# One core, windowed attention into a SoLU layer: the same 736 steps, issued in another order with other buffers and engines

## The chip, the core and the metric

The kernel runs on one core of one Trainium2 chip. The metric is the device time of one execution in microseconds (us). The core has a matrix engine (TensorE, written PE), a vector engine (VectorE, DVE), a scalar engine (ScalarE, ACT), a general engine (GpSimd, POOL) and SyncE (SP), which here only issues transfers. The engines run side by side; each takes its own instructions strictly in the order in which the program issues them, and they wait for each other by semaphores.

## The reference

Four batches of eight heads, 768 tokens, head size 64. Each query sees the keys of the last 96 positions and the first 8 keys, with a bias that falls with the distance at a slope of its own for each head. The result (3072 tokens by 512) goes through a layer whose activation is h times softmax(h), then a layer norm with gain g, then a second matrix.

```python
scores = q @ k.T / 8 - slope[h] * dist          # where kept: rel in [0, 96) or key < 8
a = softmax(scores);  x = a @ v                 # x: 3072 x 512 after joining the heads
h = x @ w_in                                    # 512 -> 1024
solu = h * softmax(h)
ln = (solu - mean(solu)) / sqrt(var(solu) + 1e-6) * g_ln
out = ln @ w_out                                # 1024 -> 512, float32
```

## The kernel before

**The plan.** The kernel first collects numbered steps in a `Plan`. A step is a Python function that issues a few instructions, with the buffers that it takes. 736 of them stand in the order of issue. Four lists, written out in the source, then fix everything that is free. `ORDER` is the order of issue, and so the order on each engine. `SLOTS` gives the index of each buffer that a step takes from a ring: 7 float32 landing buffers (`x32_`), 4 float16 ones (`x16_`), 3 and 2 for v, 5 each for the transposed q and k (`qT`, `kT`), 12 for the exponentials (`eb`), 4 for the activations (`uu`), 6 for the transposed activations (`late`), 3 output buffers (`osb`) and 8 PSUM banks (`acc`), which are taken singly or in pairs. `ENGS` names the engine of each step that may run on more than one: casts, evacuations of PSUM, squares, output scaling. `WARM` lists dummy matmuls as position:bank:count: ahead of that place of `ORDER`, so many 128x512 matmuls on a constant tile (`busy`, L1220) go to PE. Waits between engines follow from who writes and reads each buffer, so a buffer that is taken again waits for its last reader.

**The attention.** For each batch, pairs of heads of q and k come in as float32 (`load_heads` L472, `load_rows` L479), are cast to float16 (helper: ACT L266, DVE L268, POOL L270), transposed on PE (L728) and evacuated into `qT` and `kT` by the same helper. Only in batch 3 are the transposes made by DMA (L762). v comes in by `load_v` (L486) and is cast; the eight global keys' values are placed into a sparse tile `vgz` by POOL (L508), the global keys into `kg` (L516). The scores of 64-row blocks with their windows are PE work (L874, with the bias matmul L860), ACT takes the exponential (L882), some pairs are multiplied by a factor tile afterwards on DVE or POOL (`fac`, L890, two float16 operands). The scores of the global keys (L933) and their exponentials (L940) run beside that. Column sums come from PE (L954, L963), a logarithm on ACT (L970), the spread over the heads from PE (L1009), the reciprocals `rr` from an exponential on ACT (L1018). Then PE forms the weighted sums of v (L1043 for the global keys, L1053 for the windows, together called av below), DVE copies one column as a mark (`tick` L1063) and multiplies with `rr` into `xT` (L1078).

**The layer.** For each tile of 128 tokens, 24 in all: the first product (GEMM1, L1112, eight matmuls of 128x512 into a pair of banks), its exponential on ACT with the sum (`ef`, L1118), the product with h on DVE (`u`, L1121), the square with its sum on ACT (L1128) or DVE (L1132), the transpose of u, by DMA (`uturn`, L1137) or by PE (L1147), the statistics in small steps (L1167 to L1176), the second product (GEMM2, L1193, eight matmuls), its scaling on ACT (L1204) or DVE (L1207), and the store (L1211).

**The weights.** `w_in` and `w_out` come in as four transfers each (L610, L620). `w_in` is cast; `w_out` is multiplied by g (L633 to L639), its mean is formed by PE (L646) and taken away (L650).

**The queue.** All transfers, the DMA transposes among them, are issued by SP in the order of `ORDER`, so a transfer that waits for its buffer or its data holds up all behind it; only two stores at the very end are issued by ACT. A few more small steps build constant tiles at the start.

Names of steps used below: 480 is the load of a pair of q heads of batch 2; 645 is the last DMA transpose of batch 3's q and 941 the DMA transpose of an activation tile that follows it; 655 and 665 are two of the last v loads; 598 is a cast of k; 529 and 206 are exponentials of scores; 345 is a score step; 854 is one GEMM1 and 889 the exponential `ef` of another; 678 and 690 are score steps and 693 and 716 global-score steps of batch 3; 958 is a GEMM2 and 978 a GEMM1.

Of the kernel before, what the change touches and what calls it, by code (L numbers as in the profile page):

```python
# [29 lines left out]
FACT = {1, 2, 3}  # L30
SPLIT = False
ORDER = """
# [30 lines left out]
"""  # L63
SLOTS = """
# [10 lines left out]
"""  # L75
ENGS = """
# [4 lines left out]
"""  # L81
WARM = """
25:0:16 30:2:4 37:3:2 48:5:3 59:3:2 117:7:4 156:6:5
"""


# [1172 lines left out]
```

## Time and profile before

| what | value |
|---|---|
| times of three runs | 154.17, 155.07, 155.03 us |
| median | 155.03 us |
| span of the profiled execution | 154.3 us |
| PE busy | 144.9 us (94%) |
| ACT busy | 123.4 us (80%) |
| DVE busy | 119.2 us (77%) |
| POOL busy | 60.0 us (39%) |
| bytes moved | 36.35 MB in 76429 packets |

The profile is one execution on the core, and every duration below is from it. The median of the runs lies 0.7 us above its span. Times in the timeline count from the start of the span. "x8" at a row means that eight instructions in a line are shown as one; a note in brackets says how long the engine sat idle before it and which instruction or transfer ended that; "SPq" rows are the issues of SP's queue, not the transfers themselves. PE's rows are matmuls; its weight loads (PEld) run beside them.

### The profile page before, as it was taken

The page shows a single profiled execution, that of the slowest core. Times are in us where ns is not written, and L with a number is a line of the kernel's source. Part 1 is how long each engine was busy: PE and PEld are TensorE (multiplying, and loading weights), DVE is VectorE, ACT ScalarE, POOL GpSimd, SP SyncE. Part 2 cuts the span into 40 slices and gives each one's busy share as a digit, 9 for nine tenths or more (in the row PEclk, how much of TensorE's full clock was granted, in tenths as well). Part 3 has the DMA queues.
Part 4 walks back from the last instruction along what each step waited for, and adds up shares of the span by engine and source line. Part 5 has one row for each costly group of instructions (what it writes and reads, how often), then busy time and mean ns, then how long its engine had stood idle before and what let it go on. Part 6 is the DMA issues. An engine that isn't in the chain of part 4 may idle for free.

```text
span 154.3 us, 4774 instructions
## 1 busy us (share of the span) xinstructions
PE 144.9 (94%) x1877; PEld 77.9 (50%) x1877; DVE 119.2 (77%) x241; ACT 123.4 (80%) x212; POOL 60.0 (39%) x145
## 2 busy tenths in 40 slices
PE   6988899999899999799999999999999999999991
PEld 2545556477554565644544644544445644444451
DVE  6749988899999994789799959399893885799200
ACT  3959999799999888499999887878885676884642
POOL 7574456565394626852813115454212000110000
PEclk9999999999999999999999999999999999999999
DMA  4999999999996997999999999998999954488743
GB/s 146 373 305 337 307 391 327 347 340 398 295 264 108 242 285 175 220 270 233 262 196 154 271 141 244 171 233 161 189 231 259 247 141 97 90 222 223 224 166 136
DMA packets 76429, 36.35 MB, mean 236 GB/s; under 512 B 65456, under 2 KB 71928, under 8 KB 76408
## 3 DMA queue, kind: packets, MB, share of 16 engines
q1 hardware_dynamic: 76120, 35.54, 95.0%
q10 hardware_dynamic: 288, 0.52, 0.9%
q8 instruction: 14, 0.23, 0.7%
q14 instruction: 7, 0.06, 0.1%
HBM read 23.15 MB, written 6.29 MB: 191 GB/s over the span
## 4 chain that ended last, share of the span: by engine, by line
PE 44%; DMA 19%; ACT 9%; DVE 8%; POOL 7%; SPq 5%; issue 5%; POOLq 0%; DVEq 0%; ACTq 0%
PE acc L1193 16%; PE acc L1112 15%; DMA v<-in_v_dram 6%; DMA x<-in_q_dram 5%; DMA qT<-x 4%; PE acc L1053 3%; DMA kT<-x 3%; SPq L486 3%; ACT eb L882 2%; POOL x L270 2%; PE acc L728 2%; PE acc L874 2%; DVE uu L1121 2%; ACT ef L1118 2%; ACT rr L1018 1%
## 5 line engine op out<-in xcount | busy, mean ns | idle before, releaser
L1112 PE MATMUL acc<-w_in_sb,xT 128*128 128x512 f16 x192 | 44.4, 379 | 0.0
L1193 PE MATMUL acc<-gw_out_sb,late 128*128 128x512 f16 (+1 forms) x200 | 44.3, 371 | 0.1
L1121 DVE SCALAR_TENSOR_TENSOR uu<-ef,acc 128x1024 f16<-128x1024 f16 x24 | 29.2, 1216 | 5.4 <-ACT ef L1118 5.0
L882 ACT ACTIVATE eb<-acc 128x896 f16<-128x896 f32 (+1 forms) x32 | 29.3, 960 | 1.8 <-PE acc L874 1.8
L1193 PEld LDWEIGHTS <-late 128*128 128x128 f16 x200 | 18.9, 98 | 21.1 <-issue 0.9
L1118 ACT ACTIVATE ef<-acc 128x1024 f16<-128x1024 f32 x24 | 24.8, 1035 | 5.8 <-PE acc L1112 5.4
L1112 PEld LDWEIGHTS <-xT 128*128 128x128 f16 x192 | 18.1, 98 | 21.3 <-issue 1.1
L270 POOL CAST x<-x 128x768 f16<-128x768 f32 x17 | 14.4, 851 | 22.8 <-DMA x<-in_q_dram 7.8
L1078 DVE TENSOR_TENSOR xT<-acc,rr 128x384 f16<-128x384 f32 x32 | 16.3, 549 | 3.6 <-ACT rr L1018 1.9
L1053 PE MATMUL acc<-eb,v 64*64 64x160 f16 (+4 forms) x448 | 16.5, 221 | 2.1 <-DVE xT L1078 1.6
L1053 PEld LDWEIGHTS <-v 64*64 64x64 f16 x448 | 12.9, 106 | 6.6 <-issue 4.3
L1128 ACT ACTIVATE sqa<-uu 128x1024 f16<-128x1024 f16 x15 | 16.1, 1071 | 0.0
L1018 ACT ACTIVATE rr<-acc 128x768 f32<-128x768 f32 x16 | 12.7, 809 | 4.1 <-DVE tick L1063 2.5
L890 DVE TENSOR_TENSOR eb<-eb,fb 128x896 f16<-128x896 f16 (+1 forms) x19 | 14.1, 769 | 0.8 <-ACT eb L882 0.8
L270 POOL CAST v<-v 128x704 f16<-128x704 f32 (+3 forms) x13 | 8.8, 685 | 10.0 <-DMA v<-in_v_dram 9.3
L1220 PE MATMUL acc<-busy 128*128 128x512 f16 x36 | 10.8, 443 | 1.5 <-DVE busy L545 1.5
L728 PE MATMUL acc<-ident,x 128*128 128x128 f16 x144 | 11.1, 220 | 0.8 <-ACT x L266 0.7
L874 PE MATMUL acc<-qT,kT 64*64 64x160 f16 (+2 forms) x384 | 11.4, 227 | 0.3 <-ACT qT L266 0.3
L1132 DVE SCALAR_TENSOR_TENSOR sqv<-uu 128x1024 f16<-128x1024 f16 x9 | 11.5, 1277 | 0.1
L890 POOL TENSOR_TENSOR eb<-eb,fb 128x960 f16<-128x960 f16 (+1 forms) x5 | 10.4, 2081 | 2.0 <-ACT eb L882 2.0
L1043 PE MATMUL acc<-eg,vgz 64*64 64x384 f16 x64 | 10.8, 324 | 0.0
L268 DVE CAST x<-x 128x768 f16<-128x768 f32 x8 | 5.6, 709 | 6.7 <-POOL slr L371 2.3
(120 smaller groups left out, 205.7 us busy)
## 6 DMA issues: line engine op xcount, KB each, us to landing
x<-in_q_dram SPq DMA_DIRECT2D x16, 384.0 KB, 6.0
x<-in_k_dram SPq DMA_DIRECT2D x16, 384.0 KB, 5.1
out_dram<-osb SPq DMA_DIRECT2D x12, 256.0 KB, 4.7
v<-in_v_dram SPq DMA_DIRECT2D x12, 192.0 KB, 4.0
out_dram<-x SPq DMA_DIRECT2D x9, 256.0 KB, 2.2
late<-in_moe_w_in_dram SPq DMA_DIRECT2D x4, 512.0 KB, 7.4
w_out<-in_moe_w_out_dram SPq DMA_DIRECT2D x4, 512.0 KB, 6.0
v<-in_v_dram SPq DMA_DIRECT2D x12, 160.0 KB, 4.0
```

The source lines that it names most:

```text
L270: nc.gpsimd.tensor_copy(out=out, in_=in_)
L874: nc.tensor.matmul(out=sc[o : o + 64, par, col : col + n], lhsT=kk[r, BLK * c : BLK * c + BLK], rhs=qq[r, g0 : g0 + n], start=fresh, stop= ...
L882: ex["fn"] = (lambda ex=ex, qk=qk, gw=gw: nc.scalar.activation(out=eb[at(qk, "eb")][:, :, 0:gw], in_=big(qk)[:, :, 0:gw], func=AF.Exp, sca ...
L890: (nc.gpsimd if fx["at"] == "POOL" else nc.vector).tensor_tensor(out=e, in0=e, in1=fb[:, p, :, 0:gw], op=ALU.mult)
L1018: re["fn"] = lambda re=re, sp_=sp_, w=w: nc.scalar.activation(out=rr[at(re, "rr")][:, :, 0:w], in_=big(sp_)[:, :, 0:w], func=AF.Exp, scale ...
L1053: nc.tensor.matmul(out=o_[64 * h : 64 * h + 64, gl : gl + m], lhsT=vv[r, v_at(vi, h, c), pair, :], rhs=view(eb[at(e_own[b, gi, pair], "eb" ...
L1078: nc.vector.tensor_tensor(out=xT[at(xt_own[b], "xT")][:, p, q0:q1], in0=one(av, d)[:, 0:w], in1=rr[at(re, "rr")][:, d, 0:w], op=ALU.mult)
L1112: nc.tensor.matmul(out=ph()[:, ts(fh, 512)], lhsT=xT[at(xt_own[b], "xT")][:, j, ts(t % NA, P)], rhs=w_in_sb[:, j, ts(fh, 512)], start=(j = ...
L1118: ex["fn"] = lambda g1=g1, t=t, ph=ph: nc.scalar.activation(out=ef[at(g1, "ef")], in_=ph(), func=AF.Exp, accum_out=s0[:, t : t + 1])
L1121: u["fn"] = lambda u=u, g1=g1, t=t, ph=ph: nc.vector.scalar_tensor_tensor(out=uu[at(u, "uu")], in0=ef[at(g1, "ef")], scalar=USC, in1=ph(), ...
L1128: nc.scalar.activation(out=sqs_["ACT"], in_=uu[at(u, "uu")], func=AF.Square, scale=float(D_FF) ** 0.5, accum_out=s2[:, t : t + 1])
L1193: nc.tensor.matmul(out=one(g2)[:, 0:wd], lhsT=uT[at(el_o, "uT")][:, c, :], rhs=gw_out_sb[:, c, sl_], start=(c == 0), stop=(c == NFC - 1))
```

## The change

`ORDER`, `SLOTS`, `ENGS` and `WARM` are replaced; every step and every function stays. The set of steps in `ORDER` is the same. The first 61 steps of SP's queue come in the same order as before; behind these the queue is ordered anew, and so is everything on the other engines.

Decoded, the new lists give: steps on DVE 174 (176 before), on ACT 158 (158), on POOL 82 (79), on SP 140 (141; a third store goes to ACT's queue), on PE 177 (177). By kind, DVE/ACT/POOL, before and after: casts of v 4/4/12 and 0/4/16, casts of q 6/3/7 and 4/2/10, casts of k 2/4/10 and 5/2/9, casts of `w_in` 2/2/4 and 3/2/3, squares 9/15 and 8/16 (DVE/ACT), output scalings 10/15 and 11/14 (DVE/ACT), statistics 2/6 and 4/4 (DVE/POOL). Of the `fac` steps, four go from POOL to DVE (356, 509, 518, 683) and four from DVE to POOL (521, 530, 686, 692). The dummy matmuls are 32 instead of 36; five stood directly ahead of the first GEMM1 and four ahead of the first spread, where none stand now.

```diff
 ORDER = """
-126 86 12 11 271 2 13 17 16 10 15 66 14 18 0 20 73 36 3 75 7 1 4 88 68 69 89 22 53 55 56 90 8 70 38
...
-655 690 865 679 677 689 693 694 691 692 680 978 980 981 975 913 945 958 959 652 695 696 947 697 716
...
-1036 1041 1066 1037 1057 1042 1043 988 1050 1069 1070 989 990 1077 1078 1079 1071 1072 1073 952 953
-1083 1084 954 1085 1088 1089 1090
+86 66 6 73 36 53 38 79 28 18 11 2 88 52 12 10 271 3 115 60 117 92 110 5 99 13 17 15 14 0 4 9 75 279 105
...
+686 673 946 947 693 716 717 689 694 677 674 678 679 680 690 691 692 958 959 978 980 695 913 981 696 917
...
+1028 1036 1037 1065 1050 1042 1043 871 1069 1030 1031 1083 1070 1084 1078 1079 1072 1073 1085 1088 1089
+1090
 """
 SLOTS = """
-0 1 2 3 4 5 0 0 1 2 0 0 1 1 2 0 0 1 3 3 1 2 4 2 2 3 4 0 5 1 2 5 6 3 0 0 1 3 3 1 2 1 0 2 2 3 3 1 1 4
...
+3 5 0 1 2 1 2 0 1 2 4 6 0 3 3 3 0 1 0 2 1 5 7 0 2 0 2 3 4 0 5 1 2 1 4 0 4 3 3 0 2 3 0 1 1 5 1 1 0 7 2 3 7
...
 """
 ENGS = """
-1 0 0 1 1 1 1 1 2 0 2 1 0 0 2 0 1 0 1 0 0 0 1 2 2 2 1 1 2 0 0 1 1 1 1 0 1 2 2 0 2 1 2 1 0 1 0 0 1 1
...
+1 0 1 1 1 0 1 1 2 0 2 1 2 0 0 0 1 0 0 0 0 0 1 1 2 0 0 2 1 0 2 1 1 0 1 0 2 2 1 2 0 0 0 1 1 1 0 1 1 0 1 0 1
...
 """
 WARM = """
-25:0:16 30:2:4 37:3:2 48:5:3 59:3:2 117:7:4 156:6:5
+24:0:3 25:0:16 66:2:4 70:2:5 106:6:4
 """
```

75 rows, old and new, of tables (ENGS, ORDER, SLOTS) are left out of this document.

## The prediction

> **What bounds the kernel now.** I read the page first: span, busy time, slices, chain.
>
> ```profile
> span 154.3 us, 4774 instructions
> PE 144.9 (94%) x1877; PEld 77.9 (50%) x1877; DVE 119.2 (77%) x241; ACT 123.4 (80%) x212; POOL 60.0 (39%) x145
> PE   6988899999899999799999999999999999999991
> PE 44%; DMA 19%; ACT 9%; DVE 8%; POOL 7%; SPq 5%; issue 5%; POOLq 0%; DVEq 0%; ACTq 0%
> L1220 PE MATMUL acc<-busy 128*128 128x512 f16 x36 | 10.8, 443 | 1.5 <-DVE busy L545 1.5
> ```
>
> PE is busy 94%; its row of slices falls below 9 only in the first quarter, in the slices around 39 and 62 us and at the end. But the chain is only 44% PE: other engines and transfers set when PE may go on. The last row is dummy work. So the questions are where PE is idle, and what holds it there. I cut the span at PE's idle places.
>
> ```profile
> core 0: us, PE busy (x) PEld busy (x) DVE busy (x) ACT busy (x) POOL busy (x), PEclk, DMA share, GB/s
> 1.50:27.00 25.50, 23.62 (x381) 13.42 (x382) 20.09 (x58) 21.42 (x34) 15.59 (x68) 1.00 1.07 331
> 27.00:61.00 34.00, 32.76 (x490) 19.28 (x489) 31.16 (x55) 31.84 (x56) 18.85 (x28) 1.00 0.99 278
> 61.00:65.80 4.80, 3.50 (x95) 3.09 (x94) 3.82 (x9) 2.27 (x5) 4.20 (x5) 1.00 0.92 192
> 65.80:116.50 50.70, 50.70 (x608) 24.61 (x607) 42.77 (x74) 44.86 (x78) 19.21 (x36) 1.00 1.13 213
> 116.50:117.20 0.70, 0.35 (x10) 0.08 (x8) 0.10 (x1) 0.49 (x2) 0.56 (x1) 1.00 1.23 226
> 117.20:151.10 33.90, 33.90 (x310) 17.37 (x310) 20.78 (x45) 21.34 (x41) 0.83 (x4) 1.00 0.71 180
> ```
>
> Length, then busy time. Idle on PE: 25.50 - 23.62 = 1.88, then 1.24, 1.30, 0, 0.35, 0. From 65.8 to 151.1 PE has work in all but 0.35 us. Since no PE step is removed there, another order can gain only idle time and dummy work. Each stage ends at a gate, a transfer that PE waits for; what is gained ahead of a gate is lost at it unless the gate moves too.
>
> **The change, part by part.**
>
> *Dummy matmuls and the first gate.* 32 instead of 36.
>
> ```profile
> 25.92 1.24 PE L1220 MATMUL acc<-busy 128*128 128x512 f16 x5
> 26.19 0.62 ACT L266 CAST w_in_sb<-late 128x512 f16<-128x512 f32 x1 [0.26 <-DMA late<-in_moe_w_in_dram]
> 26.22 0.61 POOL L270 CAST w_in_sb<-late 128x512 f16<-128x512 f32 x1 [0.18 <-DMA late<-in_moe_w_in_dram]
> 27.00 1.89 PE L1112 MATMUL acc<-w_in_sb,xT 128*128 128x512 f16 x8
> ```
>
> The pipelined pace of such matmuls is (1.89 - 0.38) / 7 = 0.216 us, with 379 ns the duration of one. Four fewer are 0.9 us less work. But GEMM1 at 27.00 waits for the casts that end at 26.83, and these for the last part of `w_in`, whose place in the queue is among the 61 that stay. The five dummies of 25.92 only fill that wait: taking them away gains nothing. In the new order three steps of ACT (exponential 206, one global exponential, one evacuation of k) come ahead of the logarithm that stands at 26.71; score step 345 waits for 206. I put GEMM1 at 27.4, **+0.4 us**, which the idle of the next gate swallows.
>
> *The gate at 61 to 66 us.*
>
> ```profile
> 53.34 0.47 SPq L472 DMA_DIRECT2D x<-in_q_dram  x1
> 56.59 6.14 SPq L486 DMA_DIRECT2D v<-in_v_dram  x3
> 61.16 0.98 DVE L268 CAST x<-x 128x768 f16<-128x768 f32 x1 [2.12 <-DMA x<-in_q_dram]
> 62.65 0.26 PE L1053 MATMUL acc<-eb,v 64*64 64x160 f16 x2 [1.09 <-DVE xT L1078]
> 65.78 1.89 PE L1112 MATMUL acc<-w_in_sb,xT 128*128 128x512 f16 x8
> ```
>
> Load 480 is issued at 53.34 and its cast starts at 61.16, after DVE was idle 2.12 us; behind that cast stand the `xT` products that free the banks for PE, which waits 1.09. In the new queue 480 stands one place earlier, worth one neighbour's issue (0.5 to 1.4 us). But ahead of the `xT` products DVE now gets the cast of v's ends and a cast of k, and the next av takes a pair of banks that these products free. Following the new order on PE, DVE and ACT with these durations, GEMM1 of 65.78 starts at 65.7, **-0.1**. Ends: -1.30 (all idle goes) and +0.9 (480 as before, and the cast, 0.98, stands fully in the way).
>
> *74 to 80 us.*
>
> ```profile
> 74.96 1.01 ACT L1118 ACTIVATE ef<-acc 128x1024 f16<-128x1024 f32 x1
> 77.27 0.82 ACT L266 CAST x<-x 128x768 f16<-128x768 f32 x1
> 79.94 0.91 ACT L882 ACTIVATE eb<-acc 128x896 f16<-128x896 f32 x1
> ```
>
> Cast 598 (0.82, the row of such a cast) goes ahead of `ef` 889, the row at 74.96, and GEMM1 854 takes the banks that exponential 529 frees; walked through, PE has one hole of 0.3: **+0.3**, ends 0 and +0.82.
>
> *The gate at 109 us.* Here SP issues DMA transposes back to back.
>
> ```profile
> 106.31 1.24 SPq L762 DMA_TRANSPOSE qT<-x  x1
> 107.64 1.27 SPq L1137 DMA_TRANSPOSE late<-uu  x1
> DMA to landing us min/median/max: 3.1/3.2/3.3
> 107.92 0.22 POOL L516 TENSOR_TENSOR kg<-kT,hpick 128x16 f16<-128x16 f16 x1 [1.08 <-DMA kT<-x]
> 109.28 0.46 PE L874 MATMUL acc<-qT,kT 64*64 64x160 f16 x14
> ```
>
> 645, issued 106.31, lands at 106.31 + 3.2 = 109.5 by the median and 109.4 by the minimum, and the scores that read it begin at 109.28, so with no slack that the trace could show. 645 has the same place in the queue, the 108th, with the same set of transfers ahead of it. If SP needs as long for that set as before, PE can't be earlier here: whatever was won at 61 us ends at this gate. In the new order two global scores come first, then GEMM2 958, which needs transpose 941, the row at 107.64: 107.64 + 3.2 = 110.84, while its turn on PE comes at about 110.5. **+0.3**, ends 0 and +0.5.
>
> *The gate at 117 us.*
>
> ```profile
> 108.95 4.38 SPq L486 DMA_DIRECT2D v<-in_v_dram  x6
> 115.77 0.78 ACT L266 CAST v<-v 128x704 f16<-128x704 f32 x1 [0.33 <-DMA v<-in_v_dram]
> 116.29 0.77 POOL L270 CAST v<-v 128x704 f16<-128x704 f32 x1 [1.14 <-DMA v<-in_v_dram]
> 117.12 0.26 PE L1053 MATMUL acc<-eb,v 64*64 64x160 f16 x2 [0.34 <-POOL v L270]
> ```
>
> Six v loads; the last two are cast by POOL and ACT, then av starts. 655 comes one place earlier, 665 one later, so the later cast ends at about 117.1 instead of 117.06: **+0.1**, ends -0.35 and +0.7, one issue of the six (4.38 / 6 = 0.73).
>
> *The tail.* 33.90 us without a hole. Behind this gate the new order has 0.3 us more of PE work (34.0 against 33.7; a pair of steps has moved across it); the walk finds slack from 0.05 us up at each `ef`, `u` and bank. PE has that 0.3 less ahead of the gate, but there it waits in any case, so it counts: **+0.3**, ends 0 and +0.6. Removing one store from SP, the third on ACT, costs no instruction between ACT's last scalings that PE waits for: 0.
>
> *Exchanges of engines.* DVE has 50.70 - 42.77 = 7.9 us free in the long dense stage, ACT 5.8, POOL 31; three more casts on POOL, two fewer steps on DVE, even on ACT. Cover is this slack: 0. Uncovered, one cast of 0.77 shows.
>
> *The shared port.* The trace shows what the title speaks of:
>
> ```profile
> 52.60 1.04 POOL L508 TENSOR_TENSOR vgz<-vgn,pick 128x512 f16<-128x512 f32 x1
> 52.64 1.48 DVE L890 TENSOR_TENSOR eb<-eb,fb 128x896 f16<-128x896 f16 x1
> L890 DVE TENSOR_TENSOR eb<-eb,fb x19: 610/650/1482, 26.3 to 112.6; 128x896 f16<-128x896 f16 x11, 128x960 f16<-128x960 f16 x8
> ```
>
> A `fac` of 650 ns takes 1.48 beside `vgz` on POOL, 0.83 more. The Trainium skill, "SBUF — State Buffer", section "Who interferes with whom", says that DVE and GpSimd share a pair of ports, held exclusively. The row agrees for a DVE step that reads two operands; by that rule each such meeting avoided is worth 0.8 us of DVE, and the sum would be 0.8 lower for each that lay on the path. This one doesn't: DVE sits idle 2.12 us for a transfer at 61.16, and what it had saved by then would only lengthen that wait. The other meetings lie in the stage in which DVE has 7.9 us free. I take 0, with -0.8 as the low end.
>
> **Sum.** Of the rows ahead of 109 us, where SP sets the time, only what is lost at gate 109 counts: -0.1 and +0.3 are behind SP's pace, which has room of some tenths at 80 to 106; I count nothing of them. At 109 PE loses 0.3, of which the gate at 117 (0.34 idle) swallows most: 0. Then +0.1 at 117 and +0.3 in the tail: **+0.4**. Span 154.3 + 0.4 = 154.7; the median of the runs is 0.7 above the span: **155.4 us**.
>
> **The rivals.**
>
> *Faster: the queue runs freer.* For: three v loads take 6.14 us of SP's time at 56.59, one waiting for its buffer; a new order that removes this lets everything behind land 1 to 2 us earlier, at 61, 109 and 117. Against: equal sets ahead of 645, and many small-packet loads ahead of it that set the pace. It gains at most the idle 1.30 + 0.35 = 1.65, less the tail's 0.3: 155.0 - 1.35 = 153.7; with the dummies' 0.9, if the startup's gate moves too, 152.8. Chance 0.17.
>
> *Slower: the queue slips ahead of 645.* For: loads and stores that were behind (a q load from place 81 to 72, a store from 84 to 74) now stand ahead of transposes that wait for casts, and POOL holds four of these casts in a row, each behind a landing; one late cast holds up all of SP. Decides from when 645 is issued later than 106.7. Price: a slip of two transposes, 2 x 1.27 = 2.5, nothing being left behind to swallow it: 155.4 + 2.5 - 0.3 = 157.6. Chance 0.22.
>
> *Slower: the clock.* The first sixteen matmuls of the kernel show what a cold engine costs:
>
> ```profile
> 1.50 5.52 PE L1220 MATMUL acc<-busy 128*128 128x512 f16 x16 [1.50 <-DVE busy L545]
> ```
>
> 5.52 against 16 x 0.216 + 0.16 = 3.6, so 1.9 us more. If the missing dummies let PE idle long enough at 26 us, it pays this again; the gate at 61 swallows 1.3: 156.0. "TensorE: Matmul & The Clock Gate" of the Trainium skill, section "What's actually happening", gives about 3.4 us of idling for that; the longest hole I find is 1.5 us. Chance 0.03.
>
> *It does not do what it says*: the steps are the same and the lists only order them, so the waits of the hardware decide, as above; a part of the forecast's case.
>
> **How the numbers follow.** Forecast (153.9 to 156.5): 0.58; faster 0.17; queue 0.22; clock 0.03. About 1% (1.5 us) is what a measurement of this kernel can tell from no change, so faster is below 153.5, slower above 156.6. Of the faster case some two thirds lie below 153.5: 0.12. Of the queue's case nearly all lies above 156.6, with a few hundredths from the forecast's upper end: 0.24. The rest, 0.64, is within. Range 153.2 to 157.8: it takes in the faster case with the gates' idle gone, and the slip of two transposes; the 152.8 and larger slips are left out.
>
> **What would show it.** First GEMM1 at 27.2 to 27.6; the GEMM1 behind the second gate near 65.7; 645 issued within 0.4 of 106.31; GEMM2 958 near 110.9; the av at 117.1 to 117.4; 33.9 to 34.2 dense us behind it. I am wrong if 645 moves by over 1 us either way, if PE shows a hole between 80 and 106, or if an `ef` or `u` of the tail lets PE wait.

## The result and the profile after

The changed kernel takes **159.21 us** (median of four runs, 158.91 to 160.38) against 155.05 for the kernel before: ratio **1.028, 95% interval 1.021 to 1.035**. The forecast was 155.4, at most 157.8. The loss is ten times what the sum had. (Ratios are of undisturbed runs, and so can differ a little from those of the medians.)

The page of the changed kernel: span, busy time, chain.

```profile
span 157.5 us, 4745 instructions
PE 143.6 (91%) x1873; PEld 78.3 (50%) x1873; DVE 120.3 (76%) x243; ACT 123.2 (78%) x211; POOL 61.8 (39%) x144
PE 47%; DMA 22%; DVE 19%; ACT 5%; issue 4%; SPq 1%; ACTq 0%; DVEq 0%
```

The busy times have hardly moved: DVE 120.3 for 119.2, POOL 61.8 for 60.0. What has moved is the chain: DVE holds 19% of it, 8% before, and SP's queue 1%, 5% before. The span cut at the same places as before (length, then PE, PEld, DVE, ACT, POOL):

```profile
1.50:27.00 25.50, 22.65 (x375) 13.49 (x376) 20.26 (x60) 20.00 (x32) 13.43 (x49) 1.00 1.06 330
27.00:61.00 34.00, 30.19 (x477) 18.09 (x475) 29.39 (x49) 30.67 (x51) 22.69 (x36) 1.00 1.02 279
61.00:65.80 4.80, 4.80 (x102) 3.55 (x100) 4.04 (x11) 4.46 (x7) 2.27 (x6) 1.00 0.99 225
65.80:116.50 50.70, 48.32 (x584) 24.19 (x582) 42.98 (x77) 43.12 (x76) 18.78 (x28) 1.00 1.15 214
116.50:117.20 0.70, 0.70 (x5) 0.20 (x2) 0.29 (x1) 0.00 (x0) 0.70 (x1) 1.00 1.85 36
117.20:151.10 33.90, 33.90 (x325) 16.80 (x324) 22.02 (x47) 22.34 (x43) 3.12 (x7) 1.00 0.62 152
```

PE's idle time: 3.81 us from 27 to 61 (1.24 before), none at the two short gates, 2.38 in the long stage that had none before, none in the tail. Two places make the loss. Laying the two traces side by side, step by step on PE: against this first trace of before the changed kernel is 2.3 us late at 61 us, 0.6 at 66 (the kernel before had to wait at that gate anyway), 2.6 at 82, 3.5 at 101, 2.9 at the end.

The view of PE's waits names who ended them (total us, times, longest); these are the three largest behind the start that DVE ended:

```profile
PE acc L1052 <- DVE tick L1062: 1.2, 2, 0.8
PE acc L859 <- DVE uu L1120: 1.1, 2, 0.8
PE acc L1008 <- DVE l L978: 0.9, 2, 0.7
```

Now the timeline of the changed kernel at 74 to 82 us, DVE, then POOL, then PE.

```profile
74.72 1.79 DVE L1131 SCALAR_TENSOR_TENSOR sqv<-uu 128x1024 f16<-128x1024 f16 x1
76.44 2.86 DVE L889 TENSOR_TENSOR eb<-eb,fb 128x960 f16<-128x960 f16 x2
79.82 1.21 DVE L1120 SCALAR_TENSOR_TENSOR uu<-ef,acc 128x1024 f16<-128x1024 f16 x1
...
74.56 0.87 POOL L269 CAST v<-v 128x704 f16<-128x704 f32 x1 [4.33 <-DMA v<-in_v_dram]
75.40 2.85 POOL L889 TENSOR_TENSOR eb<-eb,fb 128x896 f16<-128x896 f16 x1
...
79.95 0.38 PE L873 MATMUL acc<-qT,kT 64*64 64x160 f16 x12 [0.82 <-DVE late L267]
81.09 0.22 PE L859 MATMUL acc<-bw,identb 64*64 64x64 f16 x2 [0.76 <-DVE uu L1120]
```

Two factor steps on DVE, 509 and 524, take 2.86 us together; step by step the first takes 2.32 and the second 0.61. The first ends 0.51 us after the factor step 521 on POOL (75.40 + 2.85 = 78.25). The square 899 ahead of it takes 1.80 with the read of its sum, 1.22 elsewhere. The square waits for the cast of v on POOL (until 75.43), the factor step for 521. So 1.67 + 0.58 = 2.25 us of DVE go to waiting for POOL, and the `u` step 890, which frees PE's banks, comes late by that. The trace books this waiting as busy time: a total of DVE can't show it.

At 96 us the same happens to four tiny instructions, the statistics 861, which the change moved to DVE (POOL first, then DVE, then PE):

```profile
95.76 2.55 POOL L269 CAST x<-x 128x768 f16<-128x768 f32 x3 [7.83 <-DMA qT<-x]
...
96.00 0.78 DVE L1166 TENSOR_TENSOR sq<-sums 128x6 f32<-128x6 f32 x1
96.81 0.74 DVE L1167 TENSOR_SCALAR sq<-sq 128x3 f32<-128x3 f32 x1
97.46 0.15 DVE L1168 TENSOR_TENSOR va<-sums,sq 128x3 f32<-128x3 f32 x1
97.65 0.67 DVE L1169 TENSOR_TENSOR va<-va,sq 128x3 f32<-128x3 f32 x1
98.24 1.21 DVE L1120 SCALAR_TENSOR_TENSOR uu<-ef,acc 128x1024 f16<-128x1024 f16 x1
...
100.72 0.22 PE L859 MATMUL acc<-bw,identb 64*64 64x64 f16 x2 [0.35 <-DVE uu L1120]
```

Three of the four wait, each until one of POOL's three casts has ended: 2.32 us for work that takes 0.62 where it is alone. And the queue of transfers, the rival of the prediction at nearly this time (157.6 us)? SP's issues in the changed kernel:

```profile
105.97 1.24 SPq L761 DMA_TRANSPOSE qT<-x  x1
107.31 1.25 SPq L1136 DMA_TRANSPOSE late<-uu  x1
```

645 is issued at 105.97, 0.34 us earlier than before. The queue did not slip.

### The profile page after: what moved, and what is told of

Its sections match the earlier page's. It is cut to its first block, busy times and chain, and to the rows that moved or that the text cites. A ratio compares the mean times of both kernels' runs of the same rounds, so it can differ in the third digit from the quotient of the medians.

```text
span 157.5 us, 4745 instructions
## 1 busy us (share of the span) xinstructions
PE 143.6 (91%) x1873; PEld 78.3 (50%) x1873; DVE 120.3 (76%) x243; ACT 123.2 (78%) x211; POOL 61.8 (39%) x144
## 4 chain that ended last, share of the span: by engine, by line
PE 47%; DMA 22%; DVE 19%; ACT 5%; issue 4%; SPq 1%; ACTq 0%; DVEq 0%
PE acc L1192 22%; PE acc L1111 13%; DMA late<-in_moe_w_in_dram 8%; DMA w_out<-in_moe_w_out_dram 7%; DVE uu L1120 5%; PE acc L1052 4%; DMA x<-in_k_dram 3%; DVE gw_out_sb L649 3%; DMA x<-in_q_dram 3%; DVE eb L889 3%; PE acc L953 2%; PE acc L873 1%; ACT ef L1117 1%; DVE sqv L1131 1%; PE acc L1008 1%
## 5 line engine op out<-in xcount | busy, mean ns | idle before, releaser
L881 ACT ACTIVATE eb<-acc 128x960 f16<-128x960 f32 (+1 forms) x32 | 29.1, 949 | 4.5 <-PE acc L873 4.4
L269 POOL CAST x<-x 128x768 f16<-128x768 f32 x19 | 16.7, 891 | 12.2 <-DMA qT<-x 7.8
L269 POOL CAST v<-v 128x704 f16<-128x704 f32 (+3 forms) x19 | 11.6, 628 | 15.3 <-DMA v<-in_v_dram 15.3
L1052 PE MATMUL acc<-eb,v 64*64 64x160 f16 (+4 forms) x448 | 15.5, 220 | 2.0 <-DVE tick L1062 1.2
L1127 ACT ACTIVATE sqa<-uu 128x1024 f16<-128x1024 f16 x16 | 16.8, 1051 | 0.1
L889 DVE TENSOR_TENSOR eb<-eb,fb 128x960 f16<-128x960 f16 (+1 forms) x19 | 16.0, 864 | 0.7 <-ACT eb L881 0.7
L889 POOL TENSOR_TENSOR eb<-eb,fb 128x896 f16<-128x896 f16 (+1 forms) x5 | 10.9, 2171 | 13.1 <-ACT eb L881 13.1
L873 PEld LDWEIGHTS <-kT 64*64 64x64 f16 x384 | 8.7, 106 | 5.2 <-issue 3.8
L1219 PE MATMUL acc<-busy 128*128 128x512 f16 x32 | 9.5, 459 | 1.5 <-DVE busy L544 1.5
L1131 DVE SCALAR_TENSOR_TENSOR sqv<-uu 128x1024 f16<-128x1024 f16 x8 | 10.3, 1290 | 0.1
```

Of the source, the lines that this page charges most:

```text
L269: nc.gpsimd.tensor_copy(out=out, in_=in_)
L873: nc.tensor.matmul(out=sc[o : o + 64, par, col : col + n], lhsT=kk[r, BLK * c : BLK * c + BLK], rhs=qq[r, g0 : g0 + n], start=fresh, stop= ...
L881: ex["fn"] = (lambda ex=ex, qk=qk, gw=gw: nc.scalar.activation(out=eb[at(qk, "eb")][:, :, 0:gw], in_=big(qk)[:, :, 0:gw], func=AF.Exp, sca ...
L889: (nc.gpsimd if fx["at"] == "POOL" else nc.vector).tensor_tensor(out=e, in0=e, in1=fb[:, p, :, 0:gw], op=ALU.mult)
L1052: nc.tensor.matmul(out=o_[64 * h : 64 * h + 64, gl : gl + m], lhsT=vv[r, v_at(vi, h, c), pair, :], rhs=view(eb[at(e_own[b, gi, pair], "eb" ...
L1127: nc.scalar.activation(out=sqs_["ACT"], in_=uu[at(u, "uu")], func=AF.Square, scale=float(D_FF) ** 0.5, accum_out=s2[:, t : t + 1])
```

## The experiments

The theory: DVE and POOL share a port that one of them holds for a whole instruction, and the new order sets DVE's two-operand steps beside POOL's long ones where PE waits for DVE. The rivals: DVE has too much work at that place; the dummies kept the clock up; the transfers hold PE wherever it is early. The medians of before in the same sets of runs were 154.9 to 155.2.

**One factor step off POOL.** 521 goes into a gap of DVE, 17 us earlier.

```diff
 ORDER
-... 394 376 377 395 ...  ... 529 521 530 ...
+... 394 376 521 377 395 ...  ... 529 530 ...
 ENGS of 521
-POOL
+DVE
```

> The changed kernel with one factor step, 521, taken off POOL, where it ran from 75.40 to 78.25 us, and put on DVE ahead of tick 377, where DVE sat idle from 57.38 to 59.50. DVE's own steps from 60 to 82 us stay the same, only their neighbour on POOL is gone. Theory A (shared port: the DVE factor step 509 took 2.32 us instead of 0.65 and the square 899 1.80 instead of 1.22 because POOL held the port): both fall back to 0.65 and 1.22, the u of 890 starts near 77.6 instead of 79.82, PE's holes of 0.82 and 0.76 us at 79 to 81 us go, and the kernel is 2.0 us faster than the changed one: span near 155.5, device time near 157.2. Theory B (DVE simply has too much work there, since two factor steps and a square were moved to it): the holes and the time stay within 0.5 us, span 157.0 to 157.5.

Measured: 157.43 us (ratio 1.019, interval 1.008 to 1.030), 1.8 less than the changed kernel; span 155.2. Its timeline, DVE and POOL:

```profile
75.47 1.22 DVE L1132 SCALAR_TENSOR_TENSOR sqv<-uu 128x1024 f16<-128x1024 f16 x1
76.61 1.19 DVE L890 TENSOR_TENSOR eb<-eb,fb 128x960 f16<-128x960 f16 x2
78.32 1.22 DVE L1121 SCALAR_TENSOR_TENSOR uu<-ef,acc 128x1024 f16<-128x1024 f16 x1
...
74.13 0.77 POOL L270 CAST v<-v 128x704 f16<-128x704 f32 x1 [3.14 <-DMA v<-in_v_dram]
```

The same three DVE steps as before, in the same order; without 521 beside them the two factor steps take 1.19 together. That the square takes 1.22 is luck of timing: the cast of v, for which it waited, ends here at 74.90, before the square begins. The amount of DVE work at that place is not the cause.

**Another step into the fire.** Here 521 stays on POOL and the step that paid, 509, is moved away.

```diff
 ORDER
-... 883 511 516 515 788 ...  ... 888 509 635 ...
+... 883 511 516 509 515 788 ...  ... 888 635 ...
```

> The changed kernel with DVE's factor step 509, the one that took 2.32 us, moved ahead of 515 (near 70.7 us); POOL's factor step 521 stays. Theory A (the port is held for a whole POOL instruction, and whatever two-operand step DVE has next pays): 524, which took 0.61, now takes the wait, its end stays near 78.8, so u 890 starts within 0.7 us of 79.1 and at most 1.0 us is won: span 156.5 to 157.3. Theory B (DVE has too much work there, or the step itself is slow): 890 starts at 77.5 and 2.0 us are won: span near 155.5.

Measured: 158.69 us (1.024, 1.017 to 1.031), span 157.2. DVE, then POOL:

```profile
75.02 1.79 DVE L1132 SCALAR_TENSOR_TENSOR sqv<-uu 128x1024 f16<-128x1024 f16 x1
76.74 2.29 DVE L890 TENSOR_TENSOR eb<-eb,fb 128x896 f16<-128x896 f16 x1
...
75.70 2.85 POOL L890 TENSOR_TENSOR eb<-eb,fb 128x896 f16<-128x896 f16 x1
```

Now 524 pays, 2.29 instead of 0.61, and ends 0.48 us after POOL's step. The time falls by 0.5 us, which its interval does not tell apart from the changed kernel, where theory B forecast 2.0. This is the clearest evidence: DVE's next factor step pays, whichever it is.

**The square ahead, and both.** 857 is moved ahead of xT 577, so that 861 runs before POOL's casts; then this and the first move together.

```diff
 ORDER
-... 568 569 850 577 ...  ... 937 857 581 ...
+... 568 569 850 857 577 ...  ... 937 581 ...
```

> The changed kernel with the square 857 on DVE moved ahead of xT 577, where DVE sat idle 1.65 us; the statistics 861 behind it then run before POOL's three casts of 95.76 to 98.31. Theory A (shared port: these small statistics took 2.32 us beside the casts, 0.62 where they are alone): 861 takes 0.62, u 925 starts by 96.3 instead of 98.24, PE's holes of 0.45 and 0.35 us at 99.6 and 100.7 go, and about 1.0 us is won at 101 us: span near 156.5. Theory B (the loss at 79 us is all that counts, and a gate of the transfer queue at 109 or 117 us takes back what is won at 100): span stays at 157.2 to 157.5.

> Both moves together. Theory A: they add up, 3.0 us faster than the changed kernel, span near 154.5, device time near 156.2, which leaves it 0.5 to 1.2 us slower than the kernel before, the loss that stands in the trace at 64 us. Theory B (the queue of transfers holds PE at 109 us, where it held the kernel before: transpose 645 issued at 106 lands at 109.3): the second move adds under 0.4 us to the first; span near 155.2.

Measured: the square alone 158.62 us (1.024, 1.011 to 1.038), 0.6 less than the changed kernel, not told apart from it by its interval; both together **156.28** (1.013, 1.003 to 1.023), span 154.5, as theory A had it. DVE in the run with both:

```profile
93.03 0.16 DVE L1167 TENSOR_TENSOR sq<-sums 128x6 f32<-128x6 f32 x1
93.23 0.17 DVE L1168 TENSOR_SCALAR sq<-sq 128x3 f32<-128x3 f32 x1
94.43 1.22 DVE L1121 SCALAR_TENSOR_TENSOR uu<-ef,acc 128x1024 f16<-128x1024 f16 x1 [0.77 <-ACT ef L1118]
```

PE then has no hole over 0.15 us from 57 us to the end. So some 3 of the 4 us lost (159.21 - 156.28 = 2.93 of 4.16) come back when two meetings of DVE with POOL are taken away. The second move also shifts 1.2 us of work into a gap, so its share is not the port's alone; the tiny steps' 0.16 and 0.17 for 0.78 and 0.74 are.

**The dummies back.**

```diff
 WARM
-24:0:3 25:0:16 66:2:4 70:2:5 106:6:4
+24:0:3 25:0:16 66:2:4 70:2:5 106:6:4 153:0:4 178:2:5
```

> The changed kernel with nine more dummy matmuls: five ahead of the first GEMM1 and four ahead of the first spread, where the kernel before had them. Theory A (they only fill a wait for the weights, as the prediction said): no change, 0.0 plus or minus 0.4 us, span 157.1 to 157.9. Theory C (without them PE's clock falls at 26 us and the first products run slow): 1 us or more faster.

Measured: 159.64 us (1.033, 1.025 to 1.041), span 157.8. Nothing is won; the clock rival falls, and the granted clock in the rows above is 1.00 in every stage.

**The stage from 27 to 61 us.** In the run with both moves the loss left was here: timeline of DVE, POOL, PE.

```profile
43.07 3.02 DVE L890 TENSOR_TENSOR eb<-eb,fb 128x960 f16<-128x960 f16 x2
...
43.30 2.27 POOL L890 TENSOR_TENSOR eb<-eb,fb 128x960 f16<-128x960 f16 x1 [2.30 <-ACT eb L882]
...
51.41 1.67 PE L1193 MATMUL acc<-gw_out_sb,late 128*128 128x512 f16 x7 [1.05 <-DVE gw_out_sb L650]
```

Factor step 356, moved from POOL to DVE by the change, starts while POOL's 353 runs and takes 2.46 of these 3.02. In the changed kernel's own trace 356 came first and took 0.65: a small shift in time decides which of the two engines goes first. I moved three such steps into the time when POOL is idle, then two weighings as well.

```diff
 ORDER
-... 354 265 266 ...
+... 354 265 356 350 365 266 ...
```

> The changed kernel with both earlier moves and, besides, the factor steps 356, 350 and 365 on DVE moved behind xT 265, where POOL is idle from 41.0 to 43.3 us in the run with both moves. There 356 took 2.46 us behind POOL's factor step 353, and 365 took 1.50 beside the sparse v product. Theory A (shared port): the three take 0.65 each, the eight centre steps end about 2 us earlier, PE's hole of 1.05 us ahead of the second product at 51 us goes, and PE is 1.0 to 2.0 us earlier at 60 us; since PE is without a hole behind 60 us there, as much is won at the end unless a transfer holds it: span 153.0 to 153.6, device time 154.8 to 155.4. Theory B (the transfers hold PE at 61, 109 or 117 us, as they held the kernel before): PE is earlier at 60 but waits there, and the span stays within 0.5 us of 154.5.

```diff
 ORDER
-... 160 ... 315 ...      ENGS of 158: POOL
+... 315 160 ...          ENGS of 158: ACT, behind 355
```

> As the run with the three factor steps early, and besides one weighing of w_out, 158, taken from POOL to ACT behind exponential 355 (on POOL it lay beside two such steps on DVE, 1.26 and 1.04 us instead of 0.48), and the weighing 160 on DVE moved behind the evacuation 315, for which PE waited 0.67 us at 38. Theory A: another 0.5 to 1.3 us earlier at 60 us, and a device time of 154.0 to 155.0, at or under the kernel before. Theory B (gates of the transfers): no change to the run before it, within 0.4 us.

In these two kernels 356 stands ahead of its exponential 355, so the factor of that pair is left out. Measured: 156.13 us (1.005, 1.000 to 1.010) and 156.42 (1.011, 1.004 to 1.017). The trace of the second is 1.5 us ahead of the run with both at 64 us, but then the gate of the prediction is there, on PE and SP:

```profile
110.10 1.90 PE L1193 MATMUL acc<-gw_out_sb,late 128*128 128x512 f16 x8 [0.66 <-DMA late<-uu]
...
106.89 1.25 SPq L1137 DMA_TRANSPOSE late<-uu  x1
```

941 is issued at 106.89, and the product 958 that needs it waits 0.66 until 110.10, 3.2 us later. There theory B holds, and the second of the two kernels wins nothing over the first.

**Mended, and the product behind.** 356 behind 355; then also 958 behind 978 on PE.

```diff
 ORDER
-... 354 265 356 350 365 266 ... 157 355 158 ...
+... 354 265 350 365 157 355 356 158 266 ...
```

> The run with the weights again, with the factor step 356 behind its exponential 355 as it must be (350, 365 and 356 behind xT 265; weighing 158 on ACT behind 356's place; weighing 160 behind evacuation 315; and the moves of 521 and 857). Theory A (the shared port is all of the loss, and each us won on DVE before 60 us comes out at the end): device time 154.2 to 155.2, at or under the kernel before. Theory B (once PE is early the transfers hold it again): PE is 1.5 us or more earlier than the changed kernel at 60 us, but the second product 958 waits 0.4 to 0.9 us at 110 us for the transpose 941 and av 708 waits at 116 for the last v load; 155.5 to 156.5.

```diff
 ORDER
-... 692 958 959 978 980 ...
+... 692 978 958 959 980 ...
```

> As the mended run, and besides the second product 958 put behind the first product 978 on PE, as in the kernel before, so that the transpose 941 has 1.7 us more to land. Theory B: the wait of 0.4 to 0.9 us at 110 us goes, and up to as much is won, less what av 708 then waits at 116 us: 155.0 to 156.2. Theory A: no wait there, no change, within 0.3 us of the mended run.

Measured: mended **156.2 us** (1.006, 1.001 to 1.010), span 154.0; with the product behind 156.99 (1.013, 1.007 to 1.019), span 155.2. Mended: DVE, POOL, PE; then PE of the other:

```profile
42.82 1.75 DVE L890 TENSOR_TENSOR eb<-eb,fb 128x960 f16<-128x960 f16 x3
...
44.94 2.01 POOL L890 TENSOR_TENSOR eb<-eb,fb 128x960 f16<-128x960 f16 x1 [4.05 <-ACT eb L882]
...
116.45 0.26 PE L1053 MATMUL acc<-eb,v 64*64 64x160 f16 x2 [0.19 <-ACT v L266]
```

```profile
111.52 1.67 PE L1112 MATMUL acc<-w_in_sb,xT 128*128 128x512 f16 x7 [1.49 <-ACT eb L882]
```

Three factor steps in 1.75 us, all paid at their own price. No wait at 110 us in this trace, against theory B there; a small one at 116 for v. The time is that of theory B all the same: against the run with both, 156.28, nothing is won that can be told, though 356 takes 0.64 where it took 2.46. Putting 958 behind was a mistake of mine: its product had covered the time until the exponential frees the banks of 978, and PE now waits 1.49 for them. Of the changed kernels that leave nothing out the mended one has the lowest ratio, and it is still not faster than before.

**The kernel before, again, and with its own long meeting undone.**

> The kernel before, unchanged, for a second trace and for its device time beside its span. If the time outside the span is 1.8 us, as in every run of the changed kernel, and not 0.7, the profiled execution of before on which the prediction rests lay about 1 us above the middle of its runs, and a median execution has a span near 153.4. If it is 0.7, the changed kernel lost 1.1 us outside the span.

```diff
 ORDER (of the kernel before)
-... 166 ... 807 ... 365 368 ...
+... 365 166 ... 807 ... 368 ...
```

> The kernel before with its one long meeting undone: the factor step 365, 1.48 us at 52.64 beside the sparse v product on POOL, moved ahead of the centre step 166, near 47 us, where POOL is idle. Theory A (a meeting costs time only where DVE is on the path; here DVE and PE wait for the load of q heads at 61 us anyway, as the prediction said): 365 takes 0.62 and the time stays within 0.4 us of the kernel before. Theory B (each meeting undone is worth its 0.8 us): 154.0 against 154.9.

Before again: 154.83 us; its profiled execution took 155.61 with this span, this row for the stage at the gate of 61 us, and these of DVE and POOL:

```profile
span 153.5 us, 4774 instructions
...
61.00:66.00 5.00, 4.79 (x105) 3.90 (x104) 4.17 (x9) 3.31 (x7) 2.19 (x4) 1.00 1.06 234
...
53.51 0.62 DVE L890 TENSOR_TENSOR eb<-eb,fb 128x896 f16<-128x896 f16 x1
59.64 2.15 DVE L268 CAST x<-x 128x768 f16<-128x768 f32 x1
...
59.38 2.00 POOL L890 TENSOR_TENSOR eb<-eb,fb 128x960 f16<-128x960 f16 x1
```

PE idles 0.21 us there, not 1.30 as in the first trace. The load of q heads has landed when its cast begins at 59.64, 1.5 us earlier than in the first trace; but the cast, which reads one operand, takes 2.15 us where the median of its line is 0.56, and ends 0.41 us behind POOL's factor step. And 365, the one long meeting of the first trace, takes 0.62 here. So the same kernel has its meetings at other places from one execution to the next, this gate can be made by a meeting as well as by a transfer, and a DVE step with one operand pays too. Time outside the span is 2.1 us here, 1.8 in the changed kernel's profiled run.

With the meeting undone: 155.68 us (1.006, 1.002 to 1.009), neither faster nor quite the same. DVE, then PE:

```profile
46.79 1.05 DVE L890 TENSOR_TENSOR eb<-eb,fb 128x896 f16<-128x896 f16 x1
...
51.75 1.34 DVE L979 SCALAR_TENSOR_TENSOR l<-lns,mlo 128x384 f16<-128x384 f32 x1
...
49.87 1.89 PE L1193 MATMUL acc<-gw_out_sb,late 128*128 128x512 f16 x8 [1.20 <-DVE gw_out_sb L650]
```

365 takes 1.05 at its new place, and the `split` step 373 now pays 1.34, 0.60 before. The meeting was not undone but handed on; theory A's 0.62 is a miss. Ahead of the centre steps (L650) 365 also holds these up, and PE waits 1.20 us for them, which it does in neither trace of before. That an off-path meeting is free is thus not shown by this run, and since the second trace of before has 0.62 without any move, the run was no clean test of it; it shows only that moving one step in this order is not free.

## Why the prediction was wrong

**The step that failed is "the shared port", where I took 0 with -0.8 as the low end and no high end.** The row of 1.48 against 0.65 us stood in the prediction, and so did the rule of the Trainium skill ("SBUF — State Buffer", "Who interferes with whom": a shared pair of ports, held exclusively). I used both only to ask what the change would save at a meeting that exists. I did not lay the new order of POOL beside the new order of DVE to see which meetings it makes. Nor was it so that all other meetings of before lie in the long stage: a factor step at 28.21 took 1.25 us beside POOL. The steps were listed with the change: 509 and 356 to DVE, 521 to POOL, statistics to DVE. By the traces these meetings cost about 2 us at 79 and 1 us at 100, and taking both away gave back 2.93 us. From 27 to 61 the waits alone put some 1.5 of PE's 3.81 us down to them: holes of 0.70, 0.80 and 0.22 stand right behind DVE steps of 1.07 (0.61 alone), 1.43 (0.61) and 1.39 us (0.61) beside POOL. No run shows that part by itself: in the mended run PE still idles 2.67 us there. The same section of the Trainium skill says that the one that issues first holds the pair and the other blocks fully. The runs agree, 509 ending 0.51 us behind POOL's step and 524 in its place 0.48.

**"Exchanges of engines" failed with it.** The cover was DVE's 7.9 us of free time in the long stage. DVE's busy time there is the same, 42.98 against 42.77, and PE lost 2.38: slack summed over 50 us covers nothing at the one place where `u` frees the banks. The count was off too: by the list of the change POOL gets five more casts (38 for 33), not three; three is the growth of all its steps.

**"74 to 80 us": +0.3, at most +0.82; it was +2.0.** Cast 598 went ahead of `ef` 889 as said, but the hole was made by 509 and 899 behind POOL. PE's holes at 81, 99 and 100 us are also what the prediction named as a sign of being wrong, a hole between 80 and 106.

**The stage from 27 to 61 us had no term at all.** PE's idle time rose there by 2.57. The gate at 61 gave back 1.7 of it, which is what the prediction said such a gate does; against the second trace of before, where the gate hardly holds, it is 0.6 (1.47 late at 60.98, 0.88 at 66.32).

**Right: the start.** First GEMM1 at 27.15 (forecast 27.4); the two traces of before have 27.00 and 27.82, so a term of 0.4 can't be told here. The dummies are worth nothing. (One reading was off and nothing rests on it: PE's row of slices falls below 9 at 50 to 54 us, not around 39.)

**Right in mechanism, and idle this time: the gates.** 645 within 0.4 us of 106.31, as forecast. But PE came 3 to 4 us late to 109, so nothing waited: no +0.3 there, no +0.1 at 117. Once more meetings were taken away the wait for 941 came, 0.66 us in the run with the weights and none in the mended one, which has 0.19 for v.

**Right: the tail** has no hole, 33.90 of 33.90. The +0.3 put there rested on PE waiting at the gate ahead of it, and PE did not wait; the changed kernel is 3.5 us late at 105 and 2.9 from 122 to the end.

**The span's rest.** I added 0.7 us to the span to reach the median. The time outside the span is 1.8 to 2.1; the profiled execution of before was itself about 1 us slower than the middle of its runs. In the forecast as a difference this cancels.

**The rivals.** The slip of the queue forecast 157.6 and would have been near by luck; by its own sign, the issue of 645 later than 106.7, it is refuted. The clock is refuted by the dummies. Faster: no.

What stays open is the last 0.6% between the mended kernel and the one before. Their two profiled executions are only 0.33 us apart (155.94 and 155.61). In these traces the holes of the mended kernel at 30 to 42 us are made up for by the gate of 61: its GEMM1 behind that gate starts at 65.24, that of before at 65.44. The thirteenth group of GEMM2 starts at 114.18 against 114.12, the next at 119.12 against 118.76, with the wait of 0.19 for v between them. The rest of the 0.6% stands in no trace.

## What to carry to other kernels

When an order is changed on two engines that share a port, write POOL's instructions beside DVE's with their times and look for each DVE step with all its operands in SBUF that starts while POOL is busy; its price is up to what is left of POOL's instruction, however small the DVE step is, and it comes out at the end nearly in full where PE waits for the next DVE step (1.8 of 2.25 us here). A busy share does not show it; an instruction's longest duration beside its median does. A move that undoes one meeting can make another, so read the new trace, and more than one. And a gate can forgive losses ahead of it, as that of 61 us did, so undo the late ones first.

## What the runs showed of the hardware

The rows of one line's durations (min/median/max) in the changed kernel:

```profile
L889 DVE TENSOR_TENSOR eb<-eb,fb x19: 612/653/2323, 26.0 to 115.5; 128x960 f16<-128x960 f16 x11, 128x896 f16<-128x896 f16 x8
L889 POOL TENSOR_TENSOR eb<-eb,fb x5: 1887/1887/2850, 44.8 to 116.2; 128x896 f16<-128x896 f16 x4, 128x960 f16<-128x960 f16 x1
L1166 DVE TENSOR_TENSOR sq<-sums x4: 155/161/776, 96.0 to 148.1; 128x6 f32<-128x6 f32 x4
L1120 DVE SCALAR_TENSOR_TENSOR uu<-ef,acc x24: 1205/1220/1222, 30.8 to 145.7; 128x1024 f16<-128x1024 f16 x24
```

POOL pays too: 1887 alone, 2850 where the square held the port first. A DVE instruction on 6 columns takes five times its length. And `u`, two operands of which one lies in PSUM, has the same 1.2 us in all 24 cases, though POOL was busy beside 15 of them; `xT`, which reads PSUM too, stays at 0.54 to 0.56 in every trace. The steps that got longer have all their operands in SBUF, two (509, 0.65 to 2.32) or one (the cast of the second trace of before, 0.56 to 2.15; the TENSOR_SCALAR of the statistics, 0.17 to 0.74). Not all such steps beside POOL did. Over the whole trace, against the median of the same instruction without POOL beside it, DVE's excess is about 5 us before and 9 in the changed kernel (summed from the trace); some 4 of the latter fall at 70 to 80 and 90 to 100 us.
